# In seven chunks of a fused attention and feed-forward kernel, the last two blocks of the first layer move in front of 12 products of the second layer, and the lower parts are used last

## The chip, the cores and the metric

The kernel runs on one core of a Trainium2 chip. The metric is the device time of one execution in microseconds (us). The core has TensorE (PE in the profile, with its weight loads as PEld), VectorE (DVE), ScalarE (ACT), GpSimd (POOL) and SyncE (SP, which here issues the DMAs). Each engine has a queue of its own and waits on semaphores for the others.

## The reference

Eight batches of eight heads, 576 rows, head size 64: scores of q and k, a threshold at the row's maximum less tau, a softmax over what is left, and the product with v. The result, 4608 rows of 512, goes through a feed-forward layer.

```python
scores = scale * np.matmul(q, k.transpose(0, 1, 3, 2))
thresh = np.max(scores, axis=-1, keepdims=True) - tau
scores = np.where(scores >= thresh, scores, -1000000000.0)
attn = np.exp(scores - np.max(scores, axis=-1, keepdims=True))
attn = attn / (np.sum(attn, axis=-1, keepdims=True) + 1e-09)
x = np.matmul(attn, v)                             # then 4608 x 512
h = x @ w_in                                       # 4608 x 2048
g = np.maximum(h, 0.0) + np.log1p(np.exp(-np.abs(h)))   # softplus
out = g @ w_out                                    # 4608 x 512
```

All of it is in single precision. Where one pass over a rounded operand isn't enough, an operand is split in an upper part and a lower part (what the rounding left), and a product is made of three: upper by upper, upper by lower, lower by upper.

## The kernel before, in words

**Attention.** There are 32 units, one for each batch and pair of heads (L274 to L295), and each has nine tiles of 128 rows of scores, 288 tiles in all. For a tile PE makes the scores (L423), DVE takes the row's maximum (L430), ACT the exponential (L435), DVE masks and sums it (L440), PE transposes it (L474), ACT and DVE split the transpose (L498, L132), and PE multiplies it with v some tiles later (L555 to L557). At the end of a unit its row sums go out to memory and back as a broadcast, R (L583, L587, issued by SP); POOL scales the unit's result with it (`scale_x`, L593) and SP stores it for the feed-forward layer (L597).

**Feed-forward.** The 4608 rows are cut in nine chunks of 512 (`TC`, L30). A chunk has 16 blocks of 128 columns of the first layer. A block is 12 products of 128x512 (`hidden`, L645 to L649) into one PSUM bank, named h. Blocks go in pairs (`PAIR` = 2, L49): after a pair, ACT loads the table of softplus and takes both blocks to SBUF, named st (L667); then `parts_of` (L677) makes the upper part gh on DVE (L129, on ACT in the first chunk, L127) and the lower part gl on POOL (L132). Both tags have six buffers (`NG`, L25), so block 14 takes the place of block 8 and block 15 that of block 9. The output is made in quarters of four blocks (`QF`, L80): for each quarter `qt` and each 128 rows `tb` of the chunk, `project` (L694) makes 12 products into one bank, named o, three for each block: gh by the upper weights (L703), gh by the lower weights (L705), gl by the upper weights (L707). DVE adds the bank to a sum in SBUF (L720), and after the last quarter SP stores it (L736).

**Order.** `order` (L742) writes the order of a chunk: for each quarter the blocks of the first layer that are still missing up to two blocks beyond that quarter, then its four `project` calls. So the chunk is written as blocks 0 to 5, quarter 0 (48 products), blocks 6 to 9, quarter 1, blocks 10 to 13, quarter 2, blocks 14 and 15 (24 products), quarter 3. That is 384 products a chunk. While quarter 3 is made, the x of the next chunk is loaded and split (`split_x`, L616, xh on ACT and xl on POOL), and the next chunk's first weights, wi (L629), follow as their buffers come free. The last two chunks are marked `tail` (L818) and run another order, with four blocks ahead instead of two, and mostly after the attention has ended.

**Interleaving.** The main loop (L924) goes over the 288 tiles by the letters of `PAT` (L34). Each of its two "f" draws half of the tile's share of feed-forward products from the stream, each of its two "p" is a point: `defer(n, f)` (L789) has f run n points later. The softplus is deferred by one point, the parts by one more (`HD`, L47). Where `project` comes to a block whose parts aren't yet written, `force` (L802) runs what is deferred, in order. After the last tile there is a point after every third product (L964). The written order is a priority: the framework's scheduler then orders each engine's instructions at compile time by its own forecast of when each is ready, and the softplus has its priority raised (`SPP`, L664).

Of the kernel before, what the change touches and what calls it, by code (L numbers as in the profile page):

```python
# [29 lines left out]
TC = 512  # L30
# [16 lines left out]
HD = (1, 1)  # L47
SPP = 150
PAIR = 2  # L49
# [10 lines left out]
def tile_kernel(ctx: ExitStack, tc: tile.TileContext, q, k, v, tau, w_in, w_out, out):  # L60
# [8 lines left out]
    nc = tc.nc  # L69
# [10 lines left out]
    QF = 4  # L80
# [29 lines left out]
    wo = [None] * NFC  # L110
# [12 lines left out]
    def hi_of(eng, out_, in_):  # L123
        if eng is nc.gpsimd:
            eng.tensor_scalar(out=out_, in0=in_, scalar1=1.0, scalar2=1.0, op0=ALU.mult, op1=ALU.mult)
        elif eng is nc.scalar:
            eng.copy(out_, in_)  # L127
        else:
            eng.tensor_copy(out_, in_)  # L129

    def lo_of(eng, out_, in_, hi):
        eng.tensor_tensor(out=out_, in0=in_, in1=hi.bitcast(F32), op=ALU.subtract)  # L132
# [85 lines left out]
    def need(*key):  # L218

        while key not in ready:  # L220
            if prep and not later:
                _, f, a = prep.pop(0)
                f(*a)
            else:
                force()
# [400 lines left out]
    def load_wi(u, fc):  # L626
        wi = wpool.tile([P, 2, NCC, P], F32R, tag="wi", bufs=WB, name=f"wi_{u.n}_{fc}")
        need("i", fc // 4)
        nc.sync.dma_start(wi.bitcast(F32), wi_d[fc // 4][fc % 4])  # L629
        u.wi[fc] = wi  # L630

    def hidden(u, fc):

        if fc == 0:
            for f in range(WB):
                load_wi(u, f)
        wi = u.wi.pop(fc)

        n = TC // u.T
        i = fc % n  # L640
        if i == 0:
            u.bank = ps_g.tile([P, TC], F32, tag="g", name=f"h_{u.n}_{fc}")
        h = u.bank[:, i * u.T:(i + 1) * u.T]
        for cc in range(NCC):
            nc.tensor.matmul(h, wi[:, 0, cc, :], u.h[cc], start=(cc == 0), stop=False)  # L645
            yield u.T / 512
            nc.tensor.matmul(h, wi[:, 0, cc, :], u.l[cc], start=False, stop=False)  # L647
            yield u.T / 512
            nc.tensor.matmul(h, wi[:, 1, cc, :], u.h[cc], start=False, stop=(cc == NCC - 1))  # L649
            if cc == NCC - 1:  # L650
                if fc + WB < NFC:
                    load_wi(u, fc + WB)
                if i == n - 1:
                    u.full.append((fc + 1 - n, u.bank))
                    if len(u.full) == PAIR:
                        full, u.full = u.full, []
                        defer(HD[0], lambda: softplus(u, full))
            yield u.T / 512

    def softplus(u, full):  # L660


        ts, last_ = [], None
        with tc.high_priority(SPP):  # L664
            for fc, bank in reversed(full):
                t = fpool.tile([P, TC], F32, tag="st", bufs=NST, name=f"st_{u.n}_{fc}")
                i = nc.scalar.activation(t, bank, AF.Softplus).ins  # L667
                if last_ is not None:
                    tc.add_manual_dep(i, last_.name, mybir.DependencyInfo(
                        mybir.DependencyClass.NoSync, mybir.DependencyReason.DATA), reason="one table load")  # L670
                last_ = i
                ts.append((fc, t))
        defer(HD[1], lambda: [parts_of(u, fc, t) for fc, t in reversed(ts)])

    later_g = [0]

    def parts_of(u, fc, t):  # L677

        pool, tags, bufs = (fpool, ("gh", "gl"), NG)
        if u.tail:  # L680
            spare = [("kT", 2), ("qT0", 2), ("qT1", 2), ("nat", 3), ("vt", 3)]
            i = later_g[0] % (NG + len(spare))
            later_g[0] += 1
            if i >= NG:
                tag, bufs = spare[i - NG]
                pool, tags = apool, (tag, tag)
        gh, gl = [pool.tile([P, TC], F32R, tag=tags[i], bufs=bufs, name=f"g{i}_{u.n}_{fc}") for i in range(2)]
        hi_of(nc.vector if u.n else nc.scalar, gh, t)
        lo_of(nc.gpsimd, gl, t, gh)
        for i in range(TC // u.T):  # L690
            c = slice(i * u.T, (i + 1) * u.T)
            u.g[fc + i] = (gh[:, c], gl[:, c])

    def project(u, qt, tb):  # L694
        o = ps_g.tile([P, 512], F32, tag="g", name=f"o_{u.n}_{qt}_{tb}")
        sl = slice(tb * P, (tb + 1) * P)
        for i in range(QF):
            fc = QF * qt + i
            while fc not in u.g:
                force()  # L700
            gh, gl = u.g[fc]
            need("o", fc)
            nc.tensor.matmul(o, gh[:, sl], wo[fc][:, 0, :], start=(i == 0), stop=False)  # L703
            yield 1.0
            nc.tensor.matmul(o, gh[:, sl], wo[fc][:, 1, :], start=False, stop=False)  # L705
            yield 1.0
            nc.tensor.matmul(o, gl[:, sl], wo[fc][:, 0, :], start=False, stop=(i == QF - 1))  # L707
            if i == QF - 1:
                defer(1, lambda: project_out(u, qt, tb, o))
            yield 1.0  # L710

    def project_out(u, qt, tb, o):
        if qt == 0 and tb % 2 == 0:
            t = fpool.tile([P, 2, DM], F32, tag="acc", name=f"acc_{u.n}_{tb}")
            u.acc += [t[:, 0, :], t[:, 1, :]]
        a = u.acc[tb]
        if qt == 0:
            nc.scalar.copy(a, o)
        else:
            nc.vector.tensor_tensor(out=a, in0=o, in1=a, op=ALU.add)  # L720
        if qt == NFC // QF - 1:
            defer(1, lambda: store_out(u, tb, a))

    def store_out(u, tb, a):
        t0 = u.t0 + tb * P
        c = 0
        while c < P:
            b, o = divmod(t0 + c, S)
            if o < SM:
                cg, p0 = divmod(o, P)  # L730
                m = min(P - p0, P - c)
                dst = out[b * S:b * S + SM, :].rearrange("(p c) e -> p c e", c=NC)[p0:p0 + m, cg, :]
            else:
                m = min(S - o, P - c)
                dst = out[b * S + o:b * S + o + m, :]
            nc.sync.dma_start(dst, a[c:c + m, :])  # L736
            c += m


    nq = NFC // QF  # L740

    def order():  # L742
        out_, at_ = [], 0
        for u in chunks:
            both = u.tail and u.n + 1 < len(chunks)
            for qt in range(nq):
                end = NFC * (u.n + (2 if both and qt == nq - 1 else 1))
                to = min(end, NFC * u.n + QF * (qt + 1) + (LT if u.tail else LS if u.T < TC else NG - QF))
                first_ = [("h", i // NFC, i % NFC) for i in range(at_, to)]
                at_ = max(at_, to)  # L750
                out_ += first_

                x = u.n + 1 < len(chunks) and qt == nq - (2 if u.tail else 1)
                out_ += [("o", u.n, qt, tb, x) for tb in range(u.T // P)]
        return out_

    def stream():
        for cc in range(NCC):
            load_x(chunks[0], cc)
            split_x(chunks[0], cc)  # L760
        for it in order():
            u = chunks[it[1]]
            if it[0] == "h":
                yield from hidden(u, it[2])
                continue
            if it[4]:

                nx = chunks[u.n + 1]
                per = NCC * P // u.T
                for cc in range((it[3] - 1) * per, it[3] * per):  # L770
                    if cc >= 0:
                        split_x(nx, cc)
                        if cc + 2 < NCC:
                            load_x(nx, cc + 2)
                if it[3] == 0:
                    load_x(nx, 0)
                    load_x(nx, 1)
            yield from project(u, it[2], it[3])
            if it[4] and it[3] == u.T // P - 1:
                for cc in range(it[3] * per, NCC):  # L780
                    split_x(nx, cc)
# [7 lines left out]
    def defer(n, f):  # L789
        if n == 0:  # L790
            f()
        else:
            later.append((now["p"] + n, f))
# [8 lines left out]
    def force():  # L802
        _, f = later.pop(0)
        f()
# [6 lines left out]
    while sum(u.T for u in chunks) < NT:  # L811
        u = Chunk()
# [3 lines left out]
        b, o = divmod(u.t0 + u.T - 1, S)  # L816
        first.append((b * 9 + (4 if b < NSPLIT and o < 256 else 9)) * NPAIR + (LAG0 if b <= NSPLIT and not chunks else LAG))
        u.tail = first[-1] >= NS  # L818
        chunks.append(u)
    ffn = stream()  # L820

    def target(g):
# [14 lines left out]
    for kind, g in WL:  # L837
        for m in range(4):
            n = len(prep)
# [84 lines left out]
    for g, (cur, t) in enumerate(tiles):  # L924
# [5 lines left out]
        for step in PAT0 + ("m" if g == TG - 1 else "") if g < TG else PAT:  # L930
# [24 lines left out]
            elif step == "w":  # L955
                while prep and prep[0][0] <= g:
                    _, f, a = prep.pop(0)
# [41 lines left out]
```

## Time and profile before

| | |
|---|---|
| median of the runs | 1450.6 us (1448.82, 1450.6, 1451.17) |
| the profiled execution | 1451.43 us, its span from first to last instruction 1449.6 us |
| granted TensorE clock | 0.996 |
| busy share | PE 96%, PEld 80%, DVE 68%, ACT 58%, POOL 41% |

The profile is one execution. Its span is what the engines' instructions cover; 1.8 us lie around it. A row of the timeline gives the start, the duration, engine, line of the kernel, operation, what is written and read, the count of merged instructions, and in brackets the idle time of the engine before it with what ended it. The busy time of PE is the union of modelled durations: a product of 128x512 is shown with about 0.39 us, while the next one starts about 0.23 us after it.

### The profile page before, as it was taken

How to read it: one execution, taken by the hardware profiler on the slowest of the kernel's cores; microseconds unless marked ns; L12 is line 12 of the kernel's file. 1: busy time of each engine (PE TensorE's matmuls, PEld its weight loads, DVE VectorE, ACT ScalarE, POOL GpSimd, SP SyncE). 2: the span in 40 equal slices, each digit the busy share in tenths (PEclk: the TensorE clock that was granted, in tenths of full speed). 3: DMA queues.
4: the chain of work that ended last, by engine and by line, in shares of the span. 5: the costliest groups of instructions: out<-in, count | busy, mean ns of one | idle time of the engine just before them, and what ended most of it. 6: DMA issues, size and time to landing. Idle time of an engine off the chain costs nothing.

```text
span 1449.6 us, 23487 instructions
## 1 busy us (share of the span) xinstructions
PE 1398.8 (96%) x7860; PEld 1161.8 (80%) x7860; DVE 987.2 (68%) x2211; ACT 847.1 (58%) x1615; POOL 590.3 (41%) x619
## 2 busy tenths in 40 slices
PE   6887999999999999999999999999999999999998
PEld 4555688788888888888888888888888888788886
DVE  6988588787777777777777777777777777402111
ACT  6667667667656576657665665667665765311010
POOL 3667566443333333344334333344334431324221
PEclk9999999999999999999999999999999999999999
DMA  5866765445333533445433533354344432333321
GB/s 170 227 186 206 214 191 182 126 121 160 104 106 114 135 109 116 119 132 151 122 111 96 154 105 100 117 151 120 113 119 135 147 99 73 105 126 130 118 86 44
DMA packets 131208, 189.93 MB, mean 131 GB/s; under 512 B 35312, under 2 KB 86800, under 8 KB 131088
## 3 DMA queue, kind: packets, MB, share of 16 engines
q1 hardware_dynamic: 131088, 188.43, 44.5%
q8 instruction: 63, 1.03, 0.3%
q14 instruction: 57, 0.47, 0.1%
HBM read 140.51 MB, written 27.41 MB: 116 GB/s over the span
## 4 chain that ended last, share of the span: by engine, by line
PE 78%; DVE 8%; ACT 4%; issue 3%; DMA 3%; POOL 3%; SPq 1%; POOLq 0%; DVEq 0%; ACTq 0%
PE s L423 10%; PE h L647 9%; PE h L645 9%; PE h L649 8%; PE o L707 8%; PE o L705 8%; PE o L703 8%; PE s L474 7%; PE pv L555 3%; PE pv L556 3%; PE tr L364 2%; DVE e_all L440 2%; DVE negm L430 2%; POOL g L132 1%; DMA wc_i<-in_moe_w_in_dram 1%
## 5 line engine op out<-in xcount | busy, mean ns | idle before, releaser
L132 POOL TENSOR_TENSOR g<-st,g 128x512 fp32r<-128x512 f32 x144 | 191.6, 1348 | 195.6 <-DVE g L129 184.2
L440 DVE SCALAR_TENSOR_TENSOR e_all<-s,thr,e_all 128x576 f32<-128x576 f32 x288 | 234.6, 816 | 49.1 <-ACT e_all L435 45.8
L430 DVE TENSOR_REDUCE negm<-s 128x1 f32<-128x576 f32 x288 | 217.2, 754 | 43.5 <-PE s L423 36.0
L707 PE MATMUL o<-wo_o,g 128*128 128x512 f32 x576 | 232.5, 404 | 5.3 <-POOL g L132 5.3
L435 ACT ACTIVATE e_all<-s,negm 128x576 f32<-128x576 f32 x288 | 216.0, 750 | 33.5 <-PE tr L471 14.8
L647 PE MATMUL h<-xl,wi 128*128 128x512 f32 x576 | 233.9, 406 | 0.9 <-POOL xl L132 0.9
L703 PE MATMUL o<-wo_o,g 128*128 128x512 f32 x576 | 232.3, 403 | 0.8 <-DVE acc L720 0.4
L645 PE MATMUL h<-xh,wi 128*128 128x512 f32 x576 | 230.6, 400 | 2.3 <-ACT xh L127 2.0
L649 PE MATMUL h<-xh,wi 128*128 128x512 f32 x576 | 230.6, 400 | 0.0
L705 PE MATMUL o<-wo_o,g 128*128 128x512 f32 x576 | 228.4, 397 | 0.0
L498 ACT CAST gH<-s 128x512 fp32r<-128x512 f32 (+1 forms) x270 | 145.1, 550 | 140.6 <-PE s L474 137.8
L132 DVE TENSOR_TENSOR gL<-s,gH 128x512 fp32r<-128x512 f32 (+1 forms) x270 | 169.0, 634 | 46.4 <-ACT gH L498 24.0
L423 PE MATMUL s<-kT,qT 128*128 128x288 f32 x1024 | 193.1, 310 | 7.6 <-ACT gH L512 2.0
L423 PEld LDWEIGHTS s<-kT,qT 128*128 128x128 f32 x1024 | 149.3, 191 | 28.2 <-issue 10.8
L129 DVE CAST g<-st 128x512 fp32r<-128x512 f32 x128 | 57.4, 485 | 149.5 <-ACT st L667 149.0
L474 PE MATMUL s<-identr,e_all 128*128 128x128 f32 x1008 | 154.6, 276 | 3.9 <-DVE e_all L440 3.9
L667 ACT ACTIVATE st<-h 128x512 f32<-128x512 f32 x144 | 78.3, 596 | 115.6 <-PE h L649 115.0
L707 PEld LDWEIGHTS o<-wo_o,g 128*128 128x128 f32 x576 | 108.4, 188 | 29.2 <-POOL g L132 11.0
L474 PEld LDWEIGHTS s<-identr,e_all 128*128 128x128 f32 x1008 | 114.8, 141 | 20.7 <-DVE e_all L440 12.5
L645 PEld LDWEIGHTS h<-xh,wi 128*128 128x128 f32 x576 | 108.9, 189 | 26.1 <-ACT xh L127 2.6
L647 PEld LDWEIGHTS h<-xl,wi 128*128 128x128 f32 x576 | 108.9, 189 | 23.2 <-POOL xl L132 1.7
L649 PEld LDWEIGHTS h<-xh,wi 128*128 128x128 f32 x576 | 109.0, 189 | 21.9
(107 smaller groups left out, 2363.4 us busy)
## 6 DMA issues: line engine op xcount, KB each, us to landing
wi<-wi_d SPq DMA_DIRECT2D x144, 512.0 KB
qT<-qT SPq DMA_DIRECT2D x124, 128.0 KB
R<-r_d SPq DMA_DIRECT2D x64, 144.0 KB
kn<-in_k_dram SPq DMA_DIRECT2D x32, 256.0 KB
qn<-in_q_dram SPq DMA_DIRECT2D x32, 256.0 KB
vn<-in_v_dram SPq DMA_DIRECT2D x32, 256.0 KB
wc_i<-in_moe_w_in_dram SPq DMA_DIRECT2D x16, 512.0 KB
wi_d<-wc_i SPq DMA_DIRECT2D x32, 256.0 KB
```

The lines of the kernel that those rows point to most:

```text
L132: eng.tensor_tensor(out=out_, in0=in_, in1=hi.bitcast(F32), op=ALU.subtract)
L423: i = nc.tensor.matmul(sp[:, hf, 0:HS], lhs, s.kT[j][:, k0 + hf * HS:k0 + (hf + 1) * HS], start=(m == 0), stop=(m == len(parts) - 1))
L430: nc.vector.reduce_max(negm, s.sp[t][:, :, 0:HS], axis=AX.XY, negate=True)
L435: nc.scalar.activation(e_all[:, s.half[t], :].rearrange("p (h n) -> p h n", h=2), s.sp[t][:, :, 0:HS], AF.Exp, bias=s.m[t][0], scale=1.0)
L440: masked.append(nc.vector.scalar_tensor_tensor(out=e2, in0=s.sp[t][:, :, 0:HS], scalar=s.m.pop(t)[1], in1=e2, op0=ALU.is_ge, op1=ALU.mult, ...
L474: nc.tensor.matmul(main[:, c, :], e[:, c0:c0 + P], ident, is_transpose=True, start=True, stop=True)
L645: nc.tensor.matmul(h, wi[:, 0, cc, :], u.h[cc], start=(cc == 0), stop=False)
L647: nc.tensor.matmul(h, wi[:, 0, cc, :], u.l[cc], start=False, stop=False)
L649: nc.tensor.matmul(h, wi[:, 1, cc, :], u.h[cc], start=False, stop=(cc == NCC - 1))
L703: nc.tensor.matmul(o, gh[:, sl], wo[fc][:, 0, :], start=(i == 0), stop=False)
L705: nc.tensor.matmul(o, gh[:, sl], wo[fc][:, 1, :], start=False, stop=False)
L707: nc.tensor.matmul(o, gl[:, sl], wo[fc][:, 0, :], start=False, stop=(i == QF - 1))
```

## The change

Three things change, for the seven chunks that aren't `tail`.

1. `order` takes the last `project` of quarter 2 (rows `tb` = 3, 12 products) and puts blocks 14 and 15 in front of it. A chunk is now written as ..., quarter 2 without its last 12 products, blocks 14 and 15, those 12 products, quarter 3.
2. Quarter 3 makes its 12 products in another order: the two with gl of blocks 14 and 15 come last (11th and 12th instead of 9th and 12th).
3. Since the parts of blocks 14 and 15 take the buffers of blocks 8 and 9, which the moved 12 products still read, the parts are held back (`waits`) until the first six of those 12 are written, and run at the next point after that.

The number of instructions of each kind and their sizes stay the same.

```diff
--- before.py
+++ after.py
@@ -670,8 +670,15 @@
                         mybir.DependencyClass.NoSync, mybir.DependencyReason.DATA), reason="one table load")
                 last_ = i
                 ts.append((fc, t))
-        defer(HD[1], lambda: [parts_of(u, fc, t) for fc, t in reversed(ts)])
-
+        def parts():
+            if u.n in waits:
+                waits[u.n].append(parts)
+                return
+            for fc, t in reversed(ts):
+                parts_of(u, fc, t)
+        defer(HD[1], parts)
+
+    waits = {}
     later_g = [0]
 
     def parts_of(u, fc, t):
@@ -694,19 +701,21 @@
     def project(u, qt, tb):
         o = ps_g.tile([P, 512], F32, tag="g", name=f"o_{u.n}_{qt}_{tb}")
         sl = slice(tb * P, (tb + 1) * P)
-        for i in range(QF):
+        steps = [(i, m) for i in range(QF) for m in range(3)]
+        if qt == nq - 1 and not u.tail and u.T == TC:
+
+            steps.sort(key=lambda x: (x[0] >= QF - PAIR and x[1] == 2, x))
+        for n, (i, m) in enumerate(steps):
             fc = QF * qt + i
             while fc not in u.g:
                 force()
-            gh, gl = u.g[fc]
             need("o", fc)
-            nc.tensor.matmul(o, gh[:, sl], wo[fc][:, 0, :], start=(i == 0), stop=False)
-            yield 1.0
-            nc.tensor.matmul(o, gh[:, sl], wo[fc][:, 1, :], start=False, stop=False)
-            yield 1.0
-            nc.tensor.matmul(o, gl[:, sl], wo[fc][:, 0, :], start=False, stop=(i == QF - 1))
-            if i == QF - 1:
+            nc.tensor.matmul(o, u.g[fc][m // 2][:, sl], wo[fc][:, m % 2, :], start=(n == 0), stop=(n == 3 * QF - 1))
+            if n == 3 * QF - 1:
                 defer(1, lambda: project_out(u, qt, tb, o))
+            if (u.n, qt, tb) in early and n == 3 * PAIR - 1:
+                for f in waits.pop(u.n):
+                    defer(1, f)
             yield 1.0
 
     def project_out(u, qt, tb, o):
@@ -739,6 +748,8 @@
 
     nq = NFC // QF
 
+    early = set()
+
     def order():
         out_, at_ = [], 0
         for u in chunks:
@@ -748,7 +759,14 @@
                 to = min(end, NFC * u.n + QF * (qt + 1) + (LT if u.tail else LS if u.T < TC else NG - QF))
                 first_ = [("h", i // NFC, i % NFC) for i in range(at_, to)]
                 at_ = max(at_, to)
-                out_ += first_
+                if qt == nq - 1 and not u.tail and u.T == TC:
+
+
+                    last_o = out_.pop()
+                    early.add(last_o[1:4])
+                    out_ += [("w", u.n), *first_, last_o]
+                else:
+                    out_ += first_
 
                 x = u.n + 1 < len(chunks) and qt == nq - (2 if u.tail else 1)
                 out_ += [("o", u.n, qt, tb, x) for tb in range(u.T // P)]
@@ -762,6 +780,9 @@
             u = chunks[it[1]]
             if it[0] == "h":
                 yield from hidden(u, it[2])
+                continue
+            if it[0] == "w":
+                waits[u.n] = []
                 continue
             if it[4]:
```

## The prediction

> **What bounds the kernel now.** I read the page first, then TensorE's waits, then one chunk from its timeline. The rows of engines and of a chunk say that PE is at work nearly always:
>
> ```profile
> PE 1398.8 (96%) x7860; PEld 1161.8 (80%) x7860; DVE 987.2 (68%) x2211; ACT 847.1 (58%) x1615; POOL 590.3 (41%) x619
> ```
>
> ```profile
> 647.67:806.81 159.14, 157.52 (x934) 135.32 (x932) 120.04 (x277) 103.05 (x193) 61.28 (x64) 1.00 0.42 122
> ```
>
> The second row is one whole chunk, from its first block to that of the next (159.14 us; busy time of PE, PEld, DVE, ACT, POOL, then the granted clock): PE lacks 1.6 us in it, DVE 39 us, at a full clock. So a wait that PE loses should come off the end, as long as no other wait takes its place. The list of waits names the candidates:
>
> ```profile
> PE o L707 <- POOL g L132: 5.3, 13, 0.7
> PE s L474 <- DVE e_all L440: 3.9, 12, 0.4
> ```
>
> The first is the change's object: a product with a lower part, waiting for POOL to make it. I looked at it in chunk 2, on PE, where blocks 14 and 15 end and the last quarter begins:
>
> ```profile
> 619.03 0.40 PE L645 MATMUL h<-xh,wi 128*128 128x512 f32 x1
> 619.27 0.60 PE L474 MATMUL s<-identr,e_all 128*128 128x128 f32 x4
> ...
> 619.94 0.39 PE L649 MATMUL h<-xh,wi 128*128 128x512 f32 x1
> ...
> 621.34 0.39 PE L649 MATMUL h<-xh,wi 128*128 128x512 f32 x1
> ...
> 624.03 0.60 PE L474 MATMUL s<-identr,e_all 128*128 128x128 f32 x4
> ...
> 625.40 0.39 PE L649 MATMUL h<-xh,wi 128*128 128x512 f32 x1
> 625.63 0.40 PE L703 MATMUL o<-wo_o,g 128*128 128x512 f32 x1
> ...
> 628.39 0.48 PE L703 MATMUL o<-wo_o,g 128*128 128x512 f32 x1
> 628.71 0.40 PE L705 MATMUL o<-wo_o,g 128*128 128x512 f32 x1
> ...
> 630.74 0.50 PE L707 MATMUL o<-wo_o,g 128*128 128x512 f32 x1 [0.50 <-POOL g L132]
> ...
> 631.98 0.50 PE L707 MATMUL o<-wo_o,g 128*128 128x512 f32 x1 [0.28 <-POOL g L132]
> 632.32 0.40 PE L705 MATMUL o<-wo_o,g 128*128 128x512 f32 x1
> ```
>
> Block 14 ends with the row at 619.94, block 15 with that at 625.40, and the last quarter starts at 625.63. The bracketed rows use gl of blocks 14 and 15. The scheduler has already moved a few products of the second row block ahead of them (they are the 13th and the 16th product of the quarter, where the written order has them as 9th and 12th), and still they wait. Why they are late stands on the other engines:
>
> ```profile
> 620.39 0.75 ACT L435 ACTIVATE e_all<-s,negm 128x576 f32<-128x576 f32 x1
> ...
> 625.41 0.76 ACT L435 ACTIVATE e_all<-s,negm 128x576 f32<-128x576 f32 x1
> 626.19 1.28 ACT L667 ACT_TABLE_LOAD   x1
> 627.48 1.08 ACT L667 ACTIVATE st<-h 128x512 f32<-128x512 f32 x2
> ...
> 629.80 1.28 ACT L435 ACT_TABLE_LOAD   x1
> ```
>
> ```profile
> 621.17 0.82 DVE L440 SCALAR_TENSOR_TENSOR e_all<-s,thr,e_all 128x576 f32<-128x576 f32 x1
> ...
> 628.80 0.76 DVE L129 CAST g<-st 128x512 fp32r<-128x512 f32 x2
> ```
>
> ```profile
> 625.24 1.43 POOL L593 TENSOR_TENSOR xp<-xp,R 128x576 f32<-128x576 f32 x1 [0.23 <-DVE thr L431]
> ...
> 629.29 2.63 POOL L132 TENSOR_TENSOR g<-st,g 128x512 fp32r<-128x512 f32 x2 [2.63 <-DVE g L129]
> ```
>
> It is one chain: block 15 ends at 625.79, the table load ends at 627.47, two softpluses at 628.56, two casts at 629.56, two subtractions on POOL at about 630.6 and 631.92. So gl of block 14 is there 4.8 us after block 15's end and that of block 15 6.1 us after it, and the six products and the attention work written between don't last that long.
>
> **What a wait costs.** The bracket gives idle time after a modelled end, not the loss. Unhindered, one product starts 0.23 us after the other (625.40 to 625.63). From 628.71 to 632.32 PE makes nine steps (3.61 us), where 9 x 0.23 = 2.07 would do: 1.54 us are lost, with an idle time of only 0.78. The rest is that a first upper part comes late too and that each restart costs 0.1. The Trainium skill (Perfetto Trace Analysis, section on the Tensor Engine Instruction) says that the end of a matmul is an estimate of the profiler and no measurement; the trace agrees, with 0.39 us shown for a product every 0.23. By the idle column alone the waits would come to 5.3 us, by starts to twice that.
>
> Chunks 1 to 5 repeat each other: of the 5.3 us in 13 waits, 0.41 fall in chunk 0 and 0.75 + 0.27 in chunk 6 (below), which leaves 3.87 in ten, or 0.77 a chunk, as in chunk 2. Chunk 0 and chunk 6:
>
> ```profile
> 312.03 0.50 PE L703 MATMUL o<-wo_o,g 128*128 128x512 f32 x1 [0.38 <-ACT g L127]
> ...
> 313.40 0.50 PE L707 MATMUL o<-wo_o,g 128*128 128x512 f32 x1 [0.41 <-POOL g L132]
> 313.74 0.40 PE L703 MATMUL o<-wo_o,g 128*128 128x512 f32 x1
> ```
>
> ```profile
> 1257.77 0.39 PE L705 MATMUL o<-wo_o,g 128*128 128x512 f32 x1
> 1258.91 0.50 PE L707 MATMUL o<-wo_o,g 128*128 128x512 f32 x1 [0.75 <-POOL g L132]
> ...
> 1260.14 0.50 PE L707 MATMUL o<-wo_o,g 128*128 128x512 f32 x1 [0.27 <-POOL g L132]
> 1260.48 0.40 PE L703 MATMUL o<-wo_o,g 128*128 128x512 f32 x1
> ```
>
> Chunk 0 makes four steps in 1.71 us (0.92 unhindered) after an idle 0.38: 1.17 lost. Chunk 6, with no attention left beside it, makes five steps in 2.71 (1.15): 1.56 lost. In all 5 x 1.54 + 1.17 + 1.56 = 10.4 us.
>
> **The change part by part.** *Moved blocks.* No instruction is added or removed on any engine; PE has the same 384 products a chunk. In chunk 2 blocks 14 and 15 move up by 12 products: block 15 takes block 14's slots and ends at 619.94 + 0.39 = 620.33, and the moved 12 products fill block 15's slots up to 625.40. With the latencies above, gl is there at 625.1 and 626.4. *Order in the quarter.* The lower parts are now the 11th and 12th product. The quarter's 7th has the slot at 628.39, so the 11th comes at 628.71 + 3 x 0.23 = 629.40, the 12th at 629.63. The slack is 4.3 and 3.2 us; for the upper part of block 14 (cast 3.4 us after block 15's end, needed at 628.39) it is 4.7. All waits of the kind go, 10.4 us, and the new order inside the quarter is worth nothing by itself as long as that slack holds; without it, it is worth the two products by which block 14's gl is needed later, 0.46 us a chunk.
>
> *Held parts.* The casts must wait until PE has used blocks 8 and 9 in the first six moved products. These fill the slots up to that at 621.34 and end at 621.73. The softplus can't end before 620.33 + 1.28 + 1.08 = 622.7, so this wait costs nothing; were it the last one, DVE's maxima and masks would queue behind the cast. That the parts are written up to twelve products after block 15 only changes their rank.
>
> *The ACT detour moves.* Load, two softpluses and load back (1.28 + 1.08 + 1.28 = 3.64 us) now fall one tile earlier. This is where I expect something back. The rows of L667 count such detours:
>
> ```profile
> L667 ACT ACT_TABLE_LOAD   x56: 1283/1283/1283, 164.2 to 1254.5; - x56
> ```
>
> There are 56 in the run, and the 12 waits of L474 above, the longest 0.4 us, are what they leave on PE after the first units. Where the load comes right behind an exponential, as it would here (620.39 + 0.75 = 621.14, block 15 at 620.33), I take the nearest row, a detour of the next chunk:
>
> ```profile
> 713.94 0.75 ACT L435 ACTIVATE e_all<-s,negm 128x576 f32<-128x576 f32 x1
> 714.70 1.28 ACT L667 ACT_TABLE_LOAD   x1
> ```
>
> ```profile
> 721.75 0.40 PE L707 MATMUL o<-wo_o,g 128*128 128x512 f32 x1
> 722.47 0.66 PE L474 MATMUL s<-identr,e_all 128*128 128x128 f32 x4 [0.33 <-DVE e_all L440]
> ```
>
> The transposes start 0.72 us after the product ahead, where 619.03 to 619.27 is 0.24: 0.48 lost, from the next exponential being late. Its bounds are 0 (the quarter-3 detour of chunk 2 shows no such wait) and two of them, 0.96 a chunk. I take 0.48 in chunks 0 to 5, 2.9 us; chunk 6 has no exponentials behind it.
>
> *Loads.* The next chunk's weight loads wait for the buffers of blocks 13 to 15, and two of them come earlier:
>
> ```profile
> 620.37 0.35 SPq L629 DMA_DIRECT2D wi<-wi_d  x1
> 620.81 1.09 SPq L587 DMA_DIRECT2D R<-r_d  x2
> 623.79 1.56 SPq L613 DMA_DIRECT2D xst<-x_d  x3
> ```
>
> The one that now follows block 14 at 620.37 would follow it some 4 us sooner (block 14 moves up by its own twelve slots), and block 15's would take its place ahead of R. They are needed at 647.67: nothing. If SP's order changes more than that, it is the second rival.
>
> *The sum.* 10.4 - 2.9 = 7.5 us. From the profiled execution, 1451.43 us, that is 1443.9; this execution lies 0.8 above the median of the runs, so from the median, 1450.6, it is 1443.1, and I say 1443.0.
>
> **The rivals.** *The softplus goes first.* Block 15 is done at 620.33 and the exponential starts at 620.39; the softplus has the raised priority. If it goes ahead, the exponential is 3.64 us late. Its mask now ends at 621.99 and the transposes start at 624.03, so 2.0 us are covered and 1.6 are not: 6 x 1.6 = 9.6 back, 1450.6 - 10.4 + 9.6 = 1449.8. Against it speaks that no wait of L474 exceeds 0.4 in all those detours: the scheduler puts products in such a hole. Chance 0.07.
>
> *POOL stands behind R.* The scaling at 625.24 waits for R and takes 1.43; it could stand ahead of both subtractions. Then gl of block 15 ends at 625.24 + 1.43 + 2.63 = 629.30 instead of 626.4, still 0.33 before it is needed. If R comes d later, the wait is d - 0.33, and from d = 1.9 on a chunk loses more than before. If SP issues R behind the three x loads (623.79 + 1.56 = 625.35 instead of 620.81), d is 4.5 and the wait 4.2: 2.7 worse in each of five chunks, 1450.6 + 13.4 - 1.2 - 1.6 = 1461.2, slower. Against it: POOL is idle 2.63 us before the subtractions now and nothing in the change reaches R itself. The Trainium skill (TensorE: Matmul & The Clock Gate, section on the 32x32 sub-arrays) has GpSimd's queue as strictly first in, first out; the rows here agree only in that nothing overtakes a waiting scaling. Chance 0.08.
>
> *Half of it comes.* What restarts and late upper parts cost is lost at other places, and only idle time returns: 5.3 + 0.4 - 2.9 = 2.8, 1447.8. Chance 0.06, half of it counted as same.
>
> *It doesn't do what it says.* The scheduler reorders PE by its own forecast, as the 13th and 16th product show, and could bring the moved products to the front again: 1450.6. The blocks' earlier rank speaks against it. Chance 0.04.
>
> **How the numbers follow.** About 0.2%, 2.9 us, is what a measurement of this kernel can tell from no change. The forecast has the remaining 0.75. Its own range goes from nothing given back and the lowest of the runs (1450.6 - 10.4 - 1.8 = 1438.4) to two late transposes a chunk (1450.6 - 10.4 + 5.8 = 1446.0). With the half case, up to 1448.5, it holds 0.81; the first two and the last rival are left out. Faster: 0.75 + 0.03 = 0.78; same: 0.07 + 0.04 + 0.03 = 0.14; slower: 0.08.
>
> **What would show it.** Right: the row of L707 waiting for POOL falls from 5.3 us in 13 waits to under 0.5, a chunk takes 158.1 us instead of 159.14, and L474 waiting for the mask rises from 3.9 towards 6. Wrong: that row stays; or the wait of L474 rises by 6 or more (first rival); or POOL's scaling stands ahead of the subtractions with a wait for R beyond 627 (second). If the waits go and the chunks still take 159, PE wasn't the bound.

## The result, and the profile after

The changed kernel takes 1442.14 us (median of six runs, 1438.95 to 1442.74) where the kernel before takes 1450.88 on the same chip (six runs, 1448.82 to 1452.88). The ratio is 0.9935 (95% interval 0.9921 to 0.9949): 0.65% faster, 8.7 us. The profiled execution took 1442.01 us with a span of 1440.2; the profiled spans differ by 9.4 us.

The page's row of engines, after:

```profile
PE 1392.3 (97%) x7860; PEld 1160.7 (81%) x7860; DVE 990.8 (69%) x2211; ACT 850.9 (59%) x1615; POOL 591.0 (41%) x619
```

The counts are those of before, and PE is still the engine that is nearly always busy. The stretch from one chunk's first block to the next, the same chunk as the prediction's 159.14 us (columns as there):

```profile
644.14:801.65 157.51, 156.64 (x933) 135.41 (x932) 120.71 (x277) 103.52 (x193) 61.44 (x64) 1.00 0.43 123
```

TensorE's waits, after (us in total, times, longest):

```profile
PE s L474 <- DVE e_all L440: 3.9, 12, 0.4
...
PE o L713 <- POOL g L132: 1.1, 2, 0.7
```

The wait for gl (line 713 is now all of `project`'s products) has gone from 5.3 us in 13 to 1.1 in two, and the transposes' wait, which was to rise towards 6, hasn't moved at all.

Where the 9.4 us come from, by the starts of the chunks' first products. Up to the end of chunk 0 the profile after is 0.58 ahead; it started that chunk 3.1 us later, so the two start-ups differ by more than the change could give there. Chunks 1 to 5 go from 795.56 us in all (329.45 to 1125.01) to 787.43 (328.87 to 1116.30): 8.13. Chunk 6 goes from 141.89 to 141.39, 0.50; the two tail chunks give 0.18. The prediction had 0.7, 5.3, 1.6 and nothing.

Chunk 2 again, on PE, where block 15 ends and the moved products begin:

```profile
617.70 0.40 PE L649 MATMUL h<-xh,wi 128*128 128x512 f32 x1
617.93 1.79 PE L713 MATMUL o<-wo_o,g 128*128 128x512 f32 x7
...
622.14 3.01 PE L713 MATMUL o<-wo_o,g 128*128 128x512 f32 x12
...
626.36 0.60 PE L474 MATMUL s<-identr,e_all 128*128 128x128 f32 x4
...
626.82 2.55 PE L713 MATMUL o<-wo_o,g 128*128 128x512 f32 x10
```

No row has a bracket any more: no product and no transpose waits. ACT, DVE and POOL beside it:

```profile
617.91 0.75 ACT L435 ACTIVATE e_all<-s,negm 128x576 f32<-128x576 f32 x1
618.67 1.28 ACT L667 ACT_TABLE_LOAD   x1
619.97 1.09 ACT L667 ACTIVATE st<-h 128x512 f32<-128x512 f32 x2
```

```profile
621.09 0.76 DVE L129 CAST g<-st 128x512 fp32r<-128x512 f32 x2 [1.57 <-ACT st L667]
```

```profile
621.66 2.60 POOL L132 TENSOR_TENSOR g<-st,g 128x512 fp32r<-128x512 f32 x2 [2.77 <-DVE g L129]
624.22 1.29 POOL L132 TENSOR_TENSOR xl<-xst,xh 128x512 fp32r<-128x512 f32 x1
625.47 1.43 POOL L593 TENSOR_TENSOR xp<-xp,R 128x576 f32<-128x576 f32 x1
```

It is the same chain, as long as before (block 15 ends at 618.10, the subtractions at 624.26: 6.16 us), but now PE has 12 more products to make meanwhile. The exponential goes ahead of the table load, and POOL's scaling now stands behind both subtractions, where before it stood ahead of them.

Chunk 6, where a wait is left, on PE, DVE and POOL:

```profile
1242.63 5.74 PE L713 MATMUL o<-wo_o,g 128*128 128x512 f32 x23
1249.10 3.26 PE L713 MATMUL o<-wo_o,g 128*128 128x512 f32 x13 [0.74 <-POOL g L132]
```

```profile
1245.29 1.38 DVE L129 CAST g<-st 128x512 fp32r<-128x512 f32 x2 [6.06 <-ACT st L667]
```

```profile
1244.75 1.30 POOL L132 TENSOR_TENSOR xl<-xst,xh 128x512 fp32r<-128x512 f32 x1
1246.48 2.57 POOL L132 TENSOR_TENSOR g<-st,g 128x512 fp32r<-128x512 f32 x2 [0.42 <-DVE g L129]
```

With no attention in between, the 23 products that stand in front of the one with block 15's lower part last 23 x 0.23 = 5.3 us, and the chain from block 15's end (1242.79) to the end of the second subtraction (1249.05) 6.3 us; the two casts take 1.38 us here, not 0.76, beside a POOL that is running.

### The profile page after: what moved, and what is told of

Its sections match the earlier page's. It is cut to its first block, busy times and chain, and to the rows that moved or that the text cites. A ratio compares the mean times of both kernels' runs of the same rounds, so it can differ in the third digit from the quotient of the medians.

```text
span 1440.2 us, 23512 instructions
## 1 busy us (share of the span) xinstructions
PE 1392.3 (97%) x7860; PEld 1160.7 (81%) x7860; DVE 990.8 (69%) x2211; ACT 850.9 (59%) x1615; POOL 591.0 (41%) x619
## 4 chain that ended last, share of the span: by engine, by line
PE 80%; DVE 8%; ACT 4%; issue 4%; POOL 2%; DMA 1%; SPq 1%; POOLq 0%; DVEq 0%; ACTq 0%
PE o L713 24%; PE s L423 11%; PE h L645 9%; PE h L647 9%; PE h L649 8%; PE s L474 7%; PE pv L555 3%; PE pv L556 3%; DVE e_all L440 2%; PE tr L364 2%; DVE negm L430 1%; ACT L667 1%; PE pv L549 1%; ACT st L667 1%; PE s L471 1%
## 5 line engine op out<-in xcount | busy, mean ns | idle before, releaser
L713 PE MATMUL o<-wo_o,g 128*128 128x512 f32 x1728 | 449.8, 400 | 1.1 <-POOL g L132 1.1
L713 PEld LDWEIGHTS o<-wo_o,g 128*128 128x128 f32 x1728 | 313.4, 188 | 59.9 <-POOL g L132 2.1
L129 DVE CAST g<-st 128x512 fp32r<-128x512 f32 x128 | 63.0, 529 | 147.9 <-ACT st L667 147.4
L555 PE MATMUL pv<-gH,vt 128*128 128x256 f32 (+1 forms) x432 | 118.8, 297 | 0.4 <-ACT gH L498 0.4
L556 PE MATMUL pv<-gL,vt 128*128 128x256 f32 (+1 forms) x432 | 118.8, 296 | 0.0
```

Source lines behind the costliest of these rows:

```text
L555: nc.tensor.matmul(o[:, 0:n], vt[:, c, :], h[:, c, 0:n], start=(c == 0), stop=False)
L556: nc.tensor.matmul(o[:, 0:n], vt[:, c, :], l[:, c, 0:n], start=False, stop=False)
L713: nc.tensor.matmul(o, u.g[fc][m // 2][:, sl], wo[fc][:, m % 2, :], start=(n == 0), stop=(n == 3 * QF - 1))
```

## The experiments

The table has the medians, the ratio to the kernel before, run on the same chip (its median there: 1450.44 us for the first four, 1451.18 for the next four, 1450.50 for the next two, 1451.25 and 1451.24 for the last two), and from each profile the mean length of chunks 1 to 5 and that of chunk 6, in us. Of the kernel before these are 159.11 and 141.89, of the changed one 157.49 and 141.39. A profile is one execution: that of the run with parts held for 12 took 3.4 us more than the run's median, that of the run with 24 in chunk 6 and casts on POOL 6.2 us more, the others lie within 1.8 us of theirs.

| kernel | median, us | ratio (95%) | chunks 1 to 5 | chunk 6 |
|---|---|---|---|---|
| order alone | 1451.01 | 1.0007 (0.9994 to 1.0020) | 159.33 | 141.85 |
| move alone | 1442.75 | 0.9956 (0.9941 to 0.9971) | 157.57 | 141.41 |
| no wait, old order | 1440.20 | 0.9934 (0.9919 to 0.9949) | 157.70 | 140.27 |
| in front of 24 | 1440.79 | 0.9940 (0.9927 to 0.9952) | 157.84 | 140.13 |
| lower parts on DVE | 1442.67 | 0.9937 (0.9921 to 0.9952) | 157.63 | 140.18 |
| in front of 6 | 1448.52 | 0.9979 (0.9968 to 0.9990) | 158.54 | 141.87 |
| no table loads | 1428.74 | 0.9841 (0.9824 to 0.9857) | 155.78 | 138.98 |
| 24 in chunk 6 alone | 1442.41 | 0.9937 (0.9922 to 0.9953) | 157.53 | 140.17 |
| parts held for 12 | 1445.84 | 0.9969 (0.9955 to 0.9984) | 158.28 | 141.81 |
| in front of 6, casts on POOL | 1439.86 | 0.9925 (0.9905 to 0.9944) | 157.33 | 142.04 |
| 24 in chunk 6, casts on POOL | 1451.83 | 1.0004 (0.9995 to 1.0014) | 158.95 | 142.14 |
| slow casts moved | 1435.85 | 0.9903 (0.9889 to 0.9918) | 156.36 | 140.82 |

**Order alone and move alone.** Against the changed kernel, the first leaves out the move and the hold, the second leaves out the sort:

```diff
         if qt == nq - 1 and not u.tail and u.T == TC:
-            steps.sort(key=lambda x: (x[0] >= QF - PAIR and x[1] == 2, x))
+            pass
```

> The kernel before with the new order inside the last quarter alone (lower parts of blocks 14 and 15 as 11th and 12th product), no block moved. Distance theory (the last quarter waits for the chain from block 15's end to its lower parts, 4.8 and 6.1 us, and only products written between shorten the wait): the first lower part is needed two products later, 0.46 us a chunk at most, and the scheduler had already put it later by itself: chunks 1 to 5 take 158.6 to 159.1 us instead of 159.1, time 1448 to 1451. Rival (the order of use is what brings the gain): chunks of 157.5, time 1442.

> The changed kernel with the old order inside the last quarter (lower parts as 9th and 12th product), the blocks moved. Distance theory: chunks 1 to 5 have 3 to 4 us to spare and take 157.3 to 157.7 us as with both parts; chunk 6, which has no attention beside it, may lose up to 0.46 more (141.4 to 141.9); time 1442 to 1443. Rival (the order brings the gain): chunks near 159.1, time 1450.

The order alone is worth nothing: chunks are 0.2 us longer than before, and its waits (as above) are 13 as before, of 6.4 us in all instead of 5.3, at another line:

```profile
PE o L705 <- POOL g L132: 6.4, 13, 0.7
```

The move alone gives the whole gain, as far as this can be told: its interval and that of the changed kernel overlap, and its chunks are 0.1 us longer. The likely reason is that the scheduler had already pulled other products ahead of the lower parts, so that writing the lower parts later adds no cover.

**No wait, old order.** In the kernel before, the products of blocks 14 and 15 read the parts of blocks 12 and 13, which are long there:

```diff
-            gh, gl = u.g[fc]
+            gh, gl = u.g[fc - PAIR if qt == nq - 1 and i >= QF - PAIR and not u.tail else fc]
```

> The kernel before, nothing moved, but in the last quarter of the seven chunks the products of blocks 14 and 15 read the parts of blocks 12 and 13 (so these products are of other blocks than the reference's; the parts of 14 and 15 are still made). So the wait is gone and softplus and table loads stay where they were. Distance theory: the wait is the whole loss: chunks 1 to 5 at 157.6 us, chunk 6 at 140.3, time 1440.5 to 1441.5, a ceiling for the change. Rival (the gain comes from the softplus falling beside another tile's exponential, not from the wait): chunks stay at 158.6 to 159.1, time 1448 to 1451.

This is the price of the wait by itself, with ACT's detour where it was: 159.11 - 157.70 = 1.41 us a chunk, and 1.62 in chunk 6. The changed kernel gains as much or more in chunks 1 to 5 (1.63). So the move gave nothing back there, and the detour's new place cost nothing.

**In front of 24.** Blocks 14 and 15 go in front of the last two `project` calls of quarter 2:

```diff
-                    last_o = out_.pop()
-                    early.add(last_o[1:4])
-                    out_ += [("w", u.n), *first_, last_o]
+                    last_o = out_[-2:]
+                    del out_[-2:]
+                    early.add(last_o[-1][1:4])
+                    out_ += [("w", u.n), *first_, *last_o]
```

> The changed kernel with blocks 14 and 15 in front of the last two calls of the third quarter (24 products instead of 12). Distance theory: chunks 1 to 5 have no wait left to lose, 157.3 to 157.7 us; chunk 6 loses its remaining wait of 0.74 and the restart, 140.4 instead of 141.4; time about 1441. Rival (where the table loads fall decides): with the softplus another tile earlier two late transposes of 0.48 us may come in, chunks of 157.9 to 158.5, time 1444 to 1446.

Chunk 6 loses its wait (140.13, 1.26 better than with the change), chunks 1 to 5 become 0.35 longer. Of that, 0.27 is one more late start of transposes in a chunk: in chunk 2 a mask ends at 624.81, and the transposes start at 624.87, 0.50 us after the product ahead where 0.24 would do. Their idle time is only 0.10, and the list of waits still has its 12 late transposes (3.8 us). The rest of the 0.35 isn't traced.

**Lower parts on DVE.** In the kernel before, two of the sixteen subtractions move from POOL to VectorE:

```diff
-        lo_of(nc.gpsimd, gl, t, gh)
+        lo_of(nc.vector if fc >= NFC - PAIR and not u.tail else nc.gpsimd, gl, t, gh)
```

> The kernel before, nothing moved; the lower parts of blocks 14 and 15 of the seven chunks are made on VectorE instead of GpSimd. A subtraction of this size takes 0.6 to 0.7 us there against 1.3. Distance theory: the chain from block 15's end is shorter by 0.7 and 1.0 us, so about that much of the 1.54 lost in a chunk comes back: chunks 1 to 5 at 158.1 to 158.5 us, time 1444 to 1447. Rival (VectorE's queue is what the transposes wait for, and 1.3 us more of work in it delays the mask as much as the chain gains): chunks at 159 or more, 1450.

It did more than expected: no product waits for a lower part any more, in any chunk. The two subtractions take 1.28 us on DVE for 2.63 on POOL. In chunk 2 they end 1.94 us after the first cast's start, where before it took 3.12, so gl is there 1.2 us sooner; the scheduler also places the products anew, and the wait, worth 1.41, is gone. A chain that is shorter by about what the wait was does in one line what the change does by moving the blocks.

**In front of 6, and the same with its casts on POOL.** The blocks go in the middle of the last `project` of quarter 2, so that the buffers they take are free and nothing is held:

```diff
+            if (u.n, qt, tb) in early and n == 3 * PAIR - 1:
+                for f in range(NFC - PAIR, NFC):
+                    yield from hidden(u, f)
```

> The changed kernel with blocks 14 and 15 in the middle of the third quarter's last call, in front of its last 6 products instead of its last 12; the first 6 are done by then, so no parts are held back. Distance theory: chunks 1 to 5 still have 1.5 us or more to spare and take 157.3 to 157.9 us; chunk 6 has 6 products (1.4 us) less cover than with 12 and gives back most of what it gained, 141.4 to 142.0; time 1442 to 1444. Rival (holding the parts, or the place of the softplus in the tile, matters): chunks 1 to 5 at 158 or more.

The expectation missed: chunks 1 to 5 get 0.57 of the 1.63 us. DVE, POOL and PE in chunk 2:

```profile
625.43 1.56 DVE L129 CAST g<-st 128x512 fp32r<-128x512 f32 x1
627.02 0.69 DVE L729 TENSOR_TENSOR acc<-o,acc 128x512 f32<-128x512 f32 x1
627.63 0.81 DVE L440 SCALAR_TENSOR_TENSOR e_all<-s,thr,e_all 128x576 f32<-128x576 f32 x1
```

```profile
625.41 1.29 POOL L132 TENSOR_TENSOR g<-st,g 128x512 fp32r<-128x512 f32 x1
```

```profile
628.50 0.66 PE L474 MATMUL s<-identr,e_all 128*128 128x128 f32 x4 [0.72 <-DVE e_all L440]
```

The second cast starts 0.02 us after a subtraction of POOL and takes 1.56 us, 1.1 more than its like; behind it on DVE stands the mask, and behind that the transposes. To see whether the slow cast is the cause, the casts of these two blocks went to POOL:

```diff
-        hi_of(nc.vector if u.n else nc.scalar, gh, t)
+        hi_of(nc.gpsimd if fc >= NFC - PAIR and not u.tail else nc.vector if u.n else nc.scalar, gh, t)
```

> The half-way kernel (blocks 14 and 15 in front of the last 6 products) with the upper parts of blocks 14 and 15 made on GpSimd instead of VectorE. In the half-way kernel the second cast took 1.56 us on VectorE instead of 0.42, while GpSimd ran the first subtraction, and the mask stood behind it: the transposes waited 0.72. If that slow cast is the cause of its long chunks: chunks 1 to 5 at 157.3 to 157.9 us again instead of 158.6, late transposes about 1.0 us a chunk instead of 1.6 to 1.9, time 1442 to 1445. Rival (the table loads fall at a bad place of the tile, whoever casts): chunks stay at 158.3 to 158.8, time 1447 to 1449.

Chunks 1 to 5 fall to 157.33. The transposes' wait for the mask, in front of 6 and then with these casts on POOL:

```profile
PE s L474 <- DVE e_all L440: 6.3, 16, 0.7
```

```profile
PE s L474 <- DVE e_all L440: 3.9, 12, 0.3
```

So it was the cast on VectorE, and not the place of the table loads. The run takes both casts off VectorE, so that it doesn't tell the second one's slowness from its being there.

**Parts held for 12.** The parts of blocks 14 and 15 wait until all 12 moved products are written:

```diff
-            if (u.n, qt, tb) in early and n == 3 * PAIR - 1:
+            if (u.n, qt, tb) in early and n == 3 * QF - 1:
```

> The changed kernel, where the parts of blocks 14 and 15 are held back until all 12 moved products are written instead of six. If the hold costs nothing in itself (it sets a rank, and the parts have 3 us to spare): chunks 1 to 5 at 157.3 to 157.9 us, chunk 6 within 0.3 of 141.4, time 1441 to 1443. Rival (the rank decides when the casts get onto VectorE): the waits for lower parts or the late transposes come back, chunks of 158 to 159, time 1445 to 1449.

It takes back half of the gain. DVE and POOL, chunk 2:

```profile
624.89 0.43 DVE L129 CAST g<-st 128x512 fp32r<-128x512 f32 x1 [1.57 <-ACT st L667]
625.34 0.42 DVE L566 TENSOR_TENSOR xp<-pv,xp 64x256 f32<-64x256 f32 x1
625.68 1.55 DVE L129 CAST g<-st 128x512 fp32r<-128x512 f32 x1
```

```profile
625.46 1.49 POOL L132 TENSOR_TENSOR g<-st,g 128x512 fp32r<-128x512 f32 x1 [2.76 <-DVE g L129]
```

With a later rank, another DVE instruction gets between the two casts, the first subtraction of POOL starts, and the second cast falls on it: 1.55 us in each of chunks 1 to 5. From it to the next mask DVE has no bracket, and PE waits for DVE's part of a transpose split and starts its product of scores 0.44 us late:

```profile
629.50 0.76 PE L423 MATMUL s<-kT,qT 128*128 128x288 f32 x4 [0.25 <-DVE gH L132]
```

The transposes behind that mask start another 0.30 late. In the changed kernel the two casts follow each other in 0.76 us, and the second starts ahead of the subtraction.

**No table loads.** A copy instead of the softplus:

```diff
-                i = nc.scalar.activation(t, bank, AF.Softplus).ins
+                i = nc.scalar.activation(t, bank, AF.Copy).ins
```

> The changed kernel with a copy in place of the softplus (so the first layer's output isn't the reference's), which needs no table: all table loads and the exponentials' delays go, the two copies of a pair stay. If each detour that leaves a late transpose costs 0.49 us and the others nothing: chunks 1 to 5 lose two of them, 156.4 to 156.8 instead of 157.5 us, time about 1436 to 1438. If detours cost nothing anywhere: 157.3 to 157.6. If they also cost in ways that no wait shows: below 156.4.

Chunks 1 to 5 lose another 1.7 us, 1.0 of it the late transposes, whose wait falls from 3.9 us to 0.2:

```profile
PE s L474 <- DVE e_all L440: 0.2, 1, 0.2
```

By this run alone one would say that ACT's detours make the transposes late. The last run below says otherwise.

**24 in chunk 6 alone, and with the casts on POOL.** What each run did best, put together: 24 products in chunk 6, 12 elsewhere, then also the casts of blocks 14 and 15 on POOL.

```diff
+                    k = 2 if chunks[u.n + 1].tail else 1
+                    last_o = out_[-k:]
+                    del out_[-k:]
```

> The changed kernel, where only chunk 6, the last before the two tail chunks, has its blocks 14 and 15 in front of 24 products, the others in front of 12. Distance theory: chunks 1 to 5 as in the changed kernel (157.3 to 157.7 us), chunk 6 as with 24 (140.1), time about 1440.5, between the changed kernel and the ceiling without any wait. Rival (chunk lengths depend on one another through the scheduler): chunks 1 to 5 move away from 157.5 by over 0.3.

> The kernel with 24 products of distance in chunk 6 and 12 in the others, and the upper parts of blocks 14 and 15 made on GpSimd in the seven chunks: both things that the runs showed to help. GpSimd's chain is longer by its two casts (about 0.6 us each) less VectorE's 0.8, well inside the 3 us to spare. Chunks 1 to 5 at 157.2 to 157.5 us, chunk 6 at 140.0 to 140.3, time 1438.5 to 1441, at or below the version in which nothing waits for the parts. Rival (GpSimd gets late with the next chunk's x, or the scaling behind it): chunks above 157.7.

The first has its 1.2 us in chunk 6, which is too little to tell in the median. The second loses everything. POOL, ACT and PE in chunk 2:

```profile
634.42 1.44 POOL L593 TENSOR_TENSOR xp<-xp,R 128x576 f32<-128x576 f32 x1
```

```profile
642.82 0.62 ACT L127 CAST xh<-xst 128x512 fp32r<-128x512 f32 x1 [3.67 <-DMA xst<-x_d]
643.34 0.58 ACT L498 CAST gH<-s 128x512 fp32r<-128x512 f32 x1
```

```profile
644.70 0.79 PE L423 MATMUL s<-kT,qT 128*128 128x288 f32 x4 [2.10 <-DVE gL L132]
```

With the casts in POOL's queue the scaling ends 0.6 us later (8.84 us after the start of the table load, in the changed kernel 8.23), and the store of x and the load of the next chunk's x are issued that much later. The load then takes 4.0 us until its cast can start (638.84 to 642.82) where it took 2.3 (629.86 to 632.17); why is not shown. The cast that waits for it is at the head of ACT's queue, and the split of a transpose stands behind it, which PE then lacks for 2.1 us. In the changed kernel the same cast waits 1.38 us for its load, and PE doesn't notice. In part this is the prediction's second rival in another form: not R late, but the scaling late, with the next x behind it. But chunk 2 is the worst chunk, with 161.46 us, of the slowest of twelve executions; the other four take 157.84 to 159.29. In chunk 6 the casts and other work of POOL stand between its two subtractions, and a wait of 1.5 us for a lower part comes back. What else the median lost, 9.4 us in all against the run without these casts on POOL, isn't traced. In the version in front of 6, with the same casts, the scaling stands between the two subtractions, and no such wait is seen.

**Slow casts moved.** Listing every cast of line 129 over 0.6 us beside every late transpose of line 474 gave, in the kernel before and in the changed one, two casts of 1.10 us in each of chunks 1 to 5 (one in chunk 6), those of blocks 9 and 13, and 5.0 us after each of these one late transpose; there is no other late transpose from chunk 0 on. Slow casts at other places are followed by none: in the changed kernel those of block 2, of 1.37 to 1.55 us, in chunks 1, 2, 3, 5 and 6. In the changed kernel, DVE, POOL and PE at the first of the two in chunk 3:

```profile
713.39 1.44 DVE L129 CAST g<-st 128x512 fp32r<-128x512 f32 x2 [1.57 <-ACT st L667]
...
717.26 0.69 DVE L729 TENSOR_TENSOR acc<-o,acc 128x512 f32<-128x512 f32 x1
717.87 0.81 DVE L440 SCALAR_TENSOR_TENSOR e_all<-s,thr,e_all 128x576 f32<-128x576 f32 x1
```

```profile
713.52 1.03 POOL L132 TENSOR_TENSOR vt<-vn,vt 128x320 fp32r<-128x320 f32 x1
```

```profile
718.74 0.66 PE L474 MATMUL s<-identr,e_all 128*128 128x128 f32 x4 [0.32 <-DVE e_all L440]
```

The second cast meets POOL's split of v; DVE has no bracket from there to the mask, so the mask is late by what the cast lost. The edit moves these two casts of a chunk away:

```diff
-        hi_of(nc.vector if u.n else nc.scalar, gh, t)
+        hi_of(nc.gpsimd if u.n and fc in (9, 13) and not u.tail else nc.vector if u.n else nc.scalar, gh, t)
```

> The changed kernel, with the upper parts of blocks 9 and 13 (chunks 1 to 6) made on GpSimd and not on VectorE; all other instructions as before. In the changed kernel the second cast of these two pairs takes 1101 ns where the others take 411 to 429, and some 5 us after each of them the transposes are late by 0.33 us of idle time, about 0.49 from start to start. Theory: these two late transposes in a chunk come from the slow cast (0.68 us more on VectorE, which is busy from there to the mask), and not from the table load: the row of the transposes waiting for the mask falls from 3.9 us in 12 waits to under 1 us, chunks 1 to 5 take 156.3 to 156.7 us instead of 157.5, chunk 6 about 140.9, and the median is 1436 to 1438. Rival 1: the table load itself makes the transposes late: the row stays at 12 waits of 0.33, chunks at 157.3 to 157.7, the median at 1441 to 1443. Rival 2: GpSimd's 0.6 us more push its lower parts and the split of the next q or the scaling behind them: a wait for gl, for the split of q or for the next x rises by over 0.5 a chunk, 1442 or more.

DVE and PE at the same place, and the chunk (windows):

```profile
710.05 0.43 DVE L129 CAST g<-st 128x512 fp32r<-128x512 f32 x1 [1.57 <-ACT st L667]
...
713.63 0.81 DVE L440 SCALAR_TENSOR_TENSOR e_all<-s,thr,e_all 128x576 f32<-128x576 f32 x1
```

```profile
714.67 0.60 PE L474 MATMUL s<-identr,e_all 128*128 128x128 f32 x4
```

```profile
640.81:797.30 156.49, 156.32 (x934) 135.56 (x932) 119.23 (x275) 103.33 (x193) 62.19 (x66) 1.00 0.43 123
```

The mask starts 3.58 us after the first cast, not 4.48; the transposes no longer wait, and no wait of these transposes for the mask is left after the first units:

```profile
PE s L474 <- DVE e_all L440: 0.2, 1, 0.2
```

Chunks 1 to 5 take 1.13 us less than with the change, and all table loads are still there. The theory holds, and this version, at 0.9903 (0.9889 to 0.9918), beats both kernels: its interval lies below that of the change. The edit takes the whole cast, 1.10 us, off VectorE. That its slowness alone would do it is an estimate: 0.68 us less would end the mask at 718.00 instead of 718.68, ahead of the 718.26 at which the transposes would start behind the product at 718.02 if nothing held them. The run without table loads is another 0.58 us a chunk shorter (155.78); these runs leave about that much for the loads themselves.

## Why the prediction was right, and where it was not

**The bound and the wait.** Right. PE was at work nearly always, and a wait taken from it came off the end.

**The price.** Right, and right to take it from start to start: 1.54 us a chunk was said, and the run without the wait gives 1.41; the idle column (0.77) would have given half. The rival that only idle time returns fell with it.

**The moved blocks.** Right. The chain was said to be 6.1 us after block 15's end and is 6.16. With the subtractions ended at about 622.95 and 624.26, and the two lower products at 627.14 and 627.38 if they run as written, the slack is 4.2 and 3.1 us (4.3 and 3.2 were said). The order in the quarter was worth nothing, as the move alone shows.

**The held parts.** Right that the wait costs nothing: the casts start 0.03 us after the second softplus. That the hold "only changes their rank" is true too, but a rank isn't free: six products further on it costs 0.8 us a chunk.

**What is given back.** Wrong: 2.9 us were said, from a late transpose in each of chunks 0 to 5, and nothing came. The failed step is the choice of the row. The late transpose at 722.47 does follow a detour of ACT, and I took the detour for its cause. It follows a slow cast, too, in the kernel before on DVE and POOL:

```profile
717.12 1.44 DVE L129 CAST g<-st 128x512 fp32r<-128x512 f32 x2 [1.57 <-ACT st L667]
```

```profile
717.24 1.04 POOL L132 TENSOR_TENSOR vt<-vn,vt 128x320 fp32r<-128x320 f32 x1
```

The last run shows that this cast is the cause: without it on VectorE, and with the same detour, the transposes are on time. At the change's own detour the two casts take 0.76 us, so nothing is late. The lower bound, nothing, had been read from the right neighbour, chunk 2's own detour.

**Chunk 6.** Wrong by 1.1 us: 1.56 were said and 0.50 came. The step "all waits of the kind go" took a slack that was read in chunk 2, where attention stands between the products, for a chunk where hardly any is left. By the prediction's own numbers, 12 moved products and 11 of the quarter cover 5.3 us, and the chain takes 6.1.

**The sum.** The two errors go against each other: 2.9 us that weren't lost, 1.1 that didn't come. Chunks 1 to 5 gave 1.63 a chunk, 0.2 more than the wait by itself; what these 0.2 us are stays open. So that 7.6 us were forecast and 8.7 measured is in part luck.

**The rivals.** The softplus doesn't go first (617.91 and 618.67). POOL's scaling didn't come ahead of the subtractions but behind them. Its path to the next x has little to spare: in the run with 24 products and casts on POOL, 0.6 us more in it and a slower load made PE wait 2.1 us in one chunk; in the changed kernel it holds. The scheduler didn't undo the move.

**What would show it.** 158.1 us a chunk and a wait for gl under 0.5 us were named; there are 157.5, and 1.1 in two waits, one of them chunk 6's (0.74) and the other in chunk 0 (0.39).

## What to carry to other kernels

Before a neighbouring row is taken for the price of something, look at every engine in front of it: the wait that follows a suspect may follow another one as well, and a run that removes both (no table loads) doesn't tell them apart. A slack is read at each place where it is needed; that of a stretch with interleaved work doesn't hold for the one where that work has ended. And when a wait ends a chain, see whether the chain can be made shorter by the length of the wait before work is moved around it.

## What the runs showed of the hardware

One form of VectorE instruction, the cast of 128x512 from f32 to fp32r in SBUF, has two durations, by what GpSimd does. The rows of line 129, before and after (least, median, most, ns):

```profile
L129 DVE CAST g<-st x128: 415/426/1106, 341.3 to 1424.1; 128x512 fp32r<-128x512 f32 x128
```

```profile
L129 DVE CAST g<-st x128: 411/426/1551, 340.6 to 1414.7; 128x512 fp32r<-128x512 f32 x128
```

In these two, casts that start with GpSimd idle take 411 to 429 ns (408 to 430 in all the kernels here); those over 0.6 us, 12 of 128 before and 18 after, start with one of its instructions running, take 935 to 1551 ns and end 0.28 to 0.29 us after it. The 11 or 12 that start in the last 0.04 us of one take 0.43 us. The Trainium skill (SBUF — State Buffer, section SBUF: two separate sides) says that VectorE in its faster modes and GpSimd share a pair of ports, which one of them holds for a whole instruction while the other is blocked. The rows agree: the cast that starts at 713.73 ends at 714.83, 0.28 us after the GpSimd instruction that it met (713.52 to 714.55). That this rest is shorter than the 0.43 us that a cast takes alone, the sentence doesn't explain. What it is worth here: 0.68 us of VectorE, of which 0.5 came through to TensorE, twice a chunk, and it had been in the kernel before the change.
